# Batch 2's upper projections of the first layer as quadrant products, the sums of its weights one batch earlier

## The chip, the cores and the metric

One NeuronCore of a Trainium2 chip. The metric is device time of one execution, in microseconds. Before the change: 1840.14 us, median of 3 runs (1838.12 to 1842.43). The engines are called PE (TensorE, matmuls), ACT (ScalarE), DVE (VectorE), POOL (GpSimd) and SP (SyncE, which here issues nearly all DMAs).

## The reference

Windowed attention feeds two feed-forward layers; all in float32.

```
attention, 4 batches x 8 heads x 576 x 64   (window 32; heads 4..7 with dilation 4)
x  = heads side by side                                       2304 x 512
h  = max(max(x @ w1, x @ w2), x @ w3)                         2304 x 768
x2 = h @ w_out                                                2304 x 512
P  = 8 rounds of row and column scaling of exp(x2 @ w_gate)   2304 x 8
out = sum over 8 experts e of P[:, e] * (max(x2 @ v1[e], 0) @ v2[e])
```

The change touches the line with `h` alone, for batch 2 of the batches 0 to 3. The second layer (all from 394.9 us of the trace on) is left as it is.

## The kernel before

**Arithmetic.** Each float32 operand of a large product is split into a high and a low part: ACT casts the high part, DVE or POOL subtracts it from the source (`split`, line 97). A product is three passes, high x high, high x low, low x high (`PASS`, line 389), accumulated in PSUM.

**First layer, the plain way** (`up`, `up_step`, batches 0 to 2). A batch has 576 columns of x in two halves of 288, and 6 blocks of 128 rows of h. For each block, each half and each of the three weights there are 12 matmuls of 288 columns (4 pieces of the 512 inputs x 3 passes) into one of four PSUM buffers `ps_g`. ACT copies the first weight's product, DVE takes the maximum with the second's and the third's, and the result is split into `h1`. A raw tile `raw` holds two chunks of weights, each 128 x 512; for batch 2 they are fetched again (`fetch_next`) and split by ACT and POOL into tiles `wa` (`split_next`), one every two units from unit 82 on.

**First layer by quadrants** (`up_quads`, batch 3 alone). Two blocks of one weight and the two halves of x form 2 x 2 quadrants, and seven products of 6 matmuls replace eight. The seven need combined weights S1 to S4 and combined inputs T1 to T4. `sums_w1` makes S1 to S4 of the raw weights on DVE, four sums of 256 columns for each of the 9 pairs, in staging tiles, and stores them in DRAM (`wsf`); `more_w1` fetches them in groups of two pairs and splits them (X and Y), and fetches A11, A12 and A22, which batches 0 and 1 left split in DRAM (`wsp`). `make_quad` makes T1 to T4 of the input `xf` and splits all seven quadrants into the two large tiles `spaces`. A group of two pairs takes seven steps; in a step PE makes a product for each pair, 12 matmuls. `keep` copies a partial product out of PSUM (ACT), `result` adds it to another (DVE) and takes the running maximum over the three weights in `best`; the third weight's result is put on a list, `todo`, and split after the next step. Side 0 of a pair uses `ps_g`, side 1 the two buffers `pt`, which before that serve attention.

**Order.** A unit is one step of 12 matmuls; `hooks(unit)` (line 972) is called after each and issues what other work falls due there: attention of later batches (`BEGIN`, `PARTS`, `LATE`), sums of weights (`SUMS`: fetched five units ahead, two sums at the unit, two and the store at the next), the first group's weights (`FIRST`), the quadrants of x (`QUAD`). Units 56 to 79 are batch 1's upper projections, 80 to 87 its down projection, 88 to 123 batch 2's upper, 124 to 131 its down, 132 to 167 batch 3's upper. Batch 3's attention runs in batch 2's units; k and q of a pair of heads have one buffer each, loaded again when the scores before are done. PE's order is by hand throughout. From batch 1's down projection on, ACT's and DVE's order is by hand too; before it theirs, and always POOL's and SP's, is a planner's, which places instructions by its own simulated times and by their order in the program. Every engine works its queue in order.

**Buffers.** `raw` has 4, `wa` 8, `ps_g` 4, and `cx` 3, which hold in turn staging tiles, `xf`, `best` and `x2`.

Of the kernel before, what the change touches and what calls it, by code (L numbers as in the profile page):

```python
# [26 lines left out]
BEGIN = {2: (48, 60, 67, 71), 3: (91, 98, 105, 112)}  # L27
SUMS = (86, 89, 93, 96, 100, 103, 107, 110, 114)
WEIGHTS = 78
FIRST = {118: "S", 120: "A1", 121: "A2", 122: "X0", 123: "X1", 126: "Y0", 127: "Y1"}  # L30
LATE = {
    0: "S Ma", 1: "Mb", 2: "X0", 3: "X1", 4: "X2", 5: "X3", 6: "X4", 7: "Ra Rb", 8: "W",
    10: "T0 E0 T1 E1", 11: "T2 E2", 13: "V0 H0", 14: "V1 H1",
}
QUAD = {125: ("B11",), 126: ("T1",), 128: ("T2",), 129: ("B21",), 130: ("T3",), 132: ("B22",), 133: ("T4",)}
EARLY = {
# [80 lines left out]
def attention_moe(ctx: ExitStack, tc: tile.TileContext, q, k, v, mask, wm1, wg, wm2, out):  # L117
# [64 lines left out]
    def attn_ops(b, p, pool, qt, kt):  # L182
# [147 lines left out]
        for a in range(2):  # L330
            ops[f"V{a}"] = partial(v, a)
            ops[f"H{a}"], ops[f"L{a}"] = (partial(hi, a), partial(lo, a)) if b < 3 else (partial(whole, a), list)
        return ops
# [125 lines left out]
    wsf = dram.tile([NQ1, P, 2, 512], F32, name="wsf")  # L459
    stage, sums, raw_s, quads_w, best, raw_1 = [], {}, {}, {}, {}, {}  # L460
    groups = [[(3, i) for i in range(i0, min(i0 + 2, NQ1))] for i0 in range(0, NQ1, 2)]

    def fetch_next(g):
        raw_1[g] = fetch_w1(g)

    def split_next(j):
        t = w1_tile(j // 2)
        split(nc, t[:, 0], t[:, 1], raw_1[j // 2][:, j % 2], nc.gpsimd)
        made[2].append(t)

# [4 lines left out]
    def fetch_sums(i):  # L475
        if i < 4 and i % 2 == 0:
            stage.append(cx_p.tile([P, 2, 2, 512], F32, name="stage", tag="cx"))
        raw = sums[i] = stage[i // 2 % 2][:, i % 2]
        for j in range(2):
            nc.sync.dma_start(raw[:, j], chunk(i, j))  # L480
# [16 lines left out]
    def more_w1(g, what):  # L497

        group = groups[g] if g < len(groups) else ()
        if what[0] in "XY":  # L500
            k = int(what[1])
            if k >= len(group):
                return
            x = group[k]
            row, names, sub = (0, ("S2", "S4"), nc.gpsimd) if what[0] == "X" else (1, ("S3", "S1"), nc.gpsimd if g in (2, 3) else nc.vector)
            t = wa_p.tile([P, 2, 512], F32R, name="wa")
            split(nc, t[:, 0], t[:, 1], raw_s[x][:, row], sub)
            for c, name in zip((0, 256), names):
                quads_w[x][name] = halves_w(t, c)
            return  # L510
# [24 lines left out]

    def make_quad(name):

        x = xf[3]
        b11, b12, b21, b22 = (x[:, k:k + 2, n:n + HB] for k in (0, 2) for n in (0, HB))
        o, y, z = {  # L540
            "B11": (b11, None, None), "T1": (b11, b12, b11), "T2": (b11, b22, b11), "B21": (b21, None, None),
            "T3": (b12, b22, b12), "B22": (b22, None, None), "T4": (b21, b21, b11),
        }[name]
        if y is not None:
            nc.vector.tensor_tensor(out=o, in0=y, in1=z, op=ALU.subtract)
        t = quads_x[3, name] = quad(name)
        split(nc, t[:, 0], t[:, 1], o, nc.vector)

    def up_quads(g, unit):
# [14 lines left out]
        def product(k, side, w, x, first):  # L564
            if first:
                if side:
                    ps[k][side] = ps_a.tile([P, 512], F32, name="q", tag="pt", bufs=2)[:, :HB]
                else:
                    ps[k][side] = ps_g.tile([P, 512], F32, name="ps")[:, :HB]
            w, x = quads_w[group[k]][w], quads_x[b, x]  # L570
            n = 0
            for kk in range(2):
                for wi, xi in PASS:
                    nc.tensor.matmul(  # L574
                        ps[k][side], w[:, wi, kk], x[:, xi, kk], start=(first and n == 0),
                        stop=n == 5, skip_group_check=not first,
                    )
                    n += 1
# [19 lines left out]
        def after(n):  # L598
            nonlocal unit
            due = 7 * g + n + (n == 7 and g == len(groups) - 1)  # L600
            for _, op in [x for x in todo if x[0] < due]:
# [3 lines left out]
            if n == 1:  # L605
                more_w1(g, "Y1") if g else None
                more_w1(g + 1, "S")
            for what in {2: ("A1",), 4: ("A2",), 5: ("X0",), 6: ("X1",), 7: ("Y0",)}.get(n, ()):
                more_w1(g + 1, what)
            for _ in range((n + 1) // 2 - n // 2 if len(both) == 1 else 1 + (n == 7)):  # L610
# [361 lines left out]
    def hooks(unit):  # L972
# [14 lines left out]
        for i, u in enumerate(SUMS):  # L987
            if unit == u - 5:
                fetch_sums(i)
            if unit in (u, u + 1):  # L990
                sums_w1(i, unit - u)
        for what in FIRST.get(unit, "").split():
            more_w1(0, what)
        for late, step, op in ((0, 4, fetch_next), (4, 2, split_next)):
            i, now = divmod(unit - WEIGHTS - late, step)
            if 0 <= i < 36 // step and not now:
                op(i)
        for name in QUAD.get(unit, ()):
            make_quad(name)
        for what in EARLY.get(unit, "").split():  # L1000
# [12 lines left out]
    for what, unit in list(zip(WORK, starts))[done:]:  # L1013
# [8 lines left out]
        if f == "out":  # L1022
            down(b, unit)
            if b == B - 1:
                ordered.close()
        elif b == 3:
            if f == "0":
# [592 lines left out]
```

## Time and profile before

| | |
|---|---|
| median of 3 runs | 1840.14 us |
| the profiled execution | 1839.86 us, of which the span is 1838.1 us |
| PE busy | 1823.5 us (99%) |
| DVE, ACT, POOL busy | 1348.1 us (73%), 961.8 us (52%), 602.6 us (33%) |
| mean granted clock of PE | 0.995 of 2.4 GHz |
| DMA | 454.08 MB, mean 247 GB/s |
| batch 1 upper, batch 1 down | 154.4 to 204.5 us, to 227.0 us |
| batch 2 upper, batch 2 down | to 299.5 us, to 321.9 us |
| batch 3 upper, batch 3 down | to 374.3 us, to 394.9 us |

Times of rows are microseconds from the start of the span. A row of groups has: line, engine, operation, out<-in, shapes, count | busy us, mean ns of one | idle time of the engine before them, and what ended it. Matmuls overlap, so the mean of one is longer than the time from one to the next.

### The profile page before, as it was taken

How to read it: one execution, taken by the hardware profiler on the slowest of the kernel's cores; microseconds unless marked ns; L12 is line 12 of the kernel's file. 1: busy time of each engine (PE TensorE's matmuls, PEld its weight loads, DVE VectorE, ACT ScalarE, POOL GpSimd, SP SyncE). 2: the span in 40 equal slices, each digit the busy share in tenths (PEclk: the TensorE clock that was granted, in tenths of full speed). 3: DMA queues.
4: the chain of work that ended last, by engine and by line, in shares of the span. 5: the costliest groups of instructions: out<-in, count | busy, mean ns of one | idle time of the engine just before them, and what ended most of it. 6: DMA issues, size and time to landing. Idle time of an engine off the chain costs nothing.

```text
span 1838.1 us, 33541 instructions
## 1 busy us (share of the span) xinstructions
PE 1823.5 (99%) x11659; PEld 1703.1 (93%) x11659; DVE 1348.1 (73%) x2634; ACT 961.8 (52%) x2387; POOL 602.6 (33%) x536
## 2 busy tenths in 40 slices
PE   8999999999999999999999999999999999999999
PEld 6999999999999988899999999999999999999999
DVE  6884374768766677666597778877788777887777
ACT  6554454444554444544446555565555555565554
POOL 0013243336666677766512121121211211111211
PEclk8999999999999999999999999999999999999999
DMA  9678495866766678776977766777698676786773
GB/s 252 230 227 287 149 273 199 290 238 247 256 251 250 255 265 305 280 260 248 370 248 253 237 222 231 240 241 241 231 362 271 224 235 229 228 263 221 229 233 110
DMA packets 235369, 454.08 MB, mean 247 GB/s; under 512 B 38656, under 2 KB 121664, under 8 KB 233920
## 3 DMA queue, kind: packets, MB, share of 16 engines
q1 hardware_dynamic: 232240, 449.15, 72.4%
q10 hardware_dynamic: 2960, 2.79, 0.5%
q8 instruction: 93, 1.52, 0.3%
q14 instruction: 76, 0.62, 0.1%
HBM read 320.70 MB, written 130.81 MB: 246 GB/s over the span
## 4 chain that ended last, share of the span: by engine, by line
PE 75%; DVE 3%; DMA 1%; issue 1%; ACT 1%; POOL 1%; DVEq 0%; SPq 0%; POOLq 0%
PE po L1370 25%; PE po L1479 13%; PE po L1108 11%; PE p L1479 6%; PE q L1479 6%; PE p L1159 5%; PE q L1159 5%; PE ps L574 1%; DMA raw<-in_wm 1%; PE ps L652 1%; PE q L574 1%; DVE sums L839 1%; DVE ts L878 1%; DVE h L1212 1%; ACT h L1211 0%
## 5 line engine op out<-in xcount | busy, mean ns | idle before, releaser
L1370 PE MATMUL po<-wt,hop 128*128 128x512 f32 (+1 forms) x2772 | 469.7, 331 | 0.0
L1370 PEld LDWEIGHTS po<-wt,hop 128*128 128x128 f32 x2772 | 416.5, 188 | 51.0
L100 POOL TENSOR_TENSOR wt<-raw,wt 128x256 fp32r<-128x256 f32 x192 | 163.0, 874 | 757.8 <-ACT wt L99 677.1
L100 DVE TENSOR_TENSOR hop<-r,hop 128x384 fp32r<-128x384 f32 x384 | 210.5, 584 | 147.6 <-ACT hop L99 143.9
L1108 PE MATMUL po<-wb,h 128*128 128x512 f32 x1152 | 295.4, 392 | 0.4 <-POOL wb L100 0.4
L1108 PEld LDWEIGHTS po<-wb,h 128*128 128x128 f32 x1152 | 213.4, 188 | 33.9 <-POOL wb L100 1.0
L99 ACT CAST hop<-r 128x384 fp32r<-128x384 f32 x384 | 188.8, 516 | 50.0 <-DVE r L1346 28.2
L425 PE MATMUL ps<-xt,wa 128*128 128x288 f32 x1296 | 183.5, 298 | 0.0
L425 PEld LDWEIGHTS ps<-xt,wa 128*128 128x128 f32 x1296 | 173.5, 188 | 1.9
L100 POOL TENSOR_TENSOR wa<-raw,wa 128x256 fp32r<-128x256 f32 (+1 forms) x107 | 127.8, 1198 | 119.3 <-ACT wa L99 86.9
L1493 ACT ACTIVATE r<-r 128x384 f32<-128x384 f32 x192 | 97.8, 525 | 126.1 <-DVE r L1492 126.1
L1404 DVE SCALAR_TENSOR_TENSOR acc<-po,prob,acc 128x256 f32<-128x256 f32 x249 | 106.4, 478 | 17.3 <-PE po L1370 15.7
L100 POOL TENSOR_TENSOR tw<-ts,tw 128x512 fp32r<-128x512 f32 x64 | 87.2, 1382 | 91.7 <-DVE h L1212 59.1
L1479 PE MATMUL po<-xB,wa 128*128 128x384 f32 x576 | 115.5, 336 | 0.0
L1479 PE MATMUL po<-xt,wa 128*128 128x384 f32 x576 | 115.5, 336 | 0.0
L100 POOL TENSOR_TENSOR wa<-sums,wa 128x512 fp32r<-128x512 f32 x64 | 88.7, 1403 | 45.6 <-ACT wa L99 30.9
L1479 PEld LDWEIGHTS po<-xB,wa 128*128 128x128 f32 x576 | 101.3, 188 | 0.0
L1479 PEld LDWEIGHTS po<-xt,wa 128*128 128x128 f32 x576 | 101.3, 188 | 0.0
L100 POOL TENSOR_TENSOR wb<-raw,wb 128x512 fp32r<-128x512 f32 x64 | 93.0, 1453 | 23.7 <-ACT wb L99 23.2
L839 DVE TENSOR_TENSOR sums<-raw 128x256 f32<-128x256 f32 x64 | 46.3, 723 | 66.4 <-DMA raw<-in_wm 63.8
L1340 DVE TENSOR_TENSOR r<-r,r 128x384 f32<-128x384 f32 x128 | 93.2, 728 | 2.2
L1381 ACT COPY mm<-po 128x256 f32<-128x256 f32 x144 | 49.0, 376 | 73.5 <-PE po L1370 73.5
(239 smaller groups left out, 3318.6 us busy)
## 6 DMA issues: line engine op xcount, KB each, us to landing
wa<-wsd SPq DMA_DIRECT2D x192, 512.0 KB, 4.4
wt<-wtd SPq DMA_DIRECT2D x256, 256.0 KB, 3.6
wsd<-wa SPq DMA_DIRECT2D x96, 512.0 KB, 3.3
raw<-in_wm SPq DMA_DIRECT2D x64, 512.0 KB, 4.1
wtd<-tw SPq DMA_DIRECT2D x128, 256.0 KB, 2.7
raw<-in_wm SPq DMA_DIRECT2D x128, 256.0 KB, 5.2
wa<-wsd SPq DMA_DIRECT2D x64, 256.0 KB, 4.7
cx<-in_wm SPq DMA_DIRECT2D x10, 1024.0 KB, 7.2
```

The costliest lines, as they stand in the source:

```text
L99: nc.scalar.copy(hi, src)
L100: sub.tensor_tensor(out=lo, in0=src, in1=hi.bitcast(F32), op=ALU.subtract)
L425: nc.tensor.matmul(ps, w[:, wi, kk], xt[:, xi, kk, n0:n0 + HB], start=(n == 0), stop=(n == 3 * KT - 1),)
L839: nc.vector.tensor_tensor(out=s[:, o], in0=x, in1=y, op=op)
L1108: nc.tensor.matmul(po, self.hs[f, j][:, hi, t * P:(t + 1) * P], self.ws[f][:, wi], start=(n + f + k == 0), stop=(n == NPAIR - 1 and f == 1 ...
L1159: nc.tensor.matmul(ps, wo[w][:, wi, kk], xo[x][:, xi, kk], start=(first and k == 0), stop=True if k == 5 else False, skip_group_check=not ...
L1340: nc.vector.tensor_tensor(out=r[o, n], in0=r[x, n], in1=r[y, n], op=op)
L1370: nc.tensor.matmul(self.ps[side, t][:, 0:x.shape[-1]], h[:, hi, t * P:(t + 1) * P], x, start=(first and i == 0), stop=(n == NPAIR - 1 and ...
L1381: nc.scalar.copy(m, self.ps[ORD[k][0], t][:, 0:256])
L1404: nc.vector.scalar_tensor_tensor(out=a, in0=src, scalar=g, in1=a, op0=ALU.mult, op1=ALU.add)
L1479: nc.tensor.matmul(ps[k][side], wo[k][w][:, wi, kk], xo[x][:, xi, kk], start=(first and c == 0), stop=c == 5, skip_group_check=not first,)
L1493: nc.scalar.activation(out=r, in_=r, func=AF.Relu)
```

## The change

Batch 2's upper projections take the way of batch 3. The groups become ten, five for each batch. The sums of the weights are made at units 61 to 84 instead of 86 to 115, in `raw` tiles instead of staging tiles; the fetch and split of batch 2's plain weights goes. Batch 2's attention result is copied whole into `xf` and its quadrants are made at units 80 to 87. In batch 2 both sides of a pair use `ps_g`, and side 1 keeps its buffer for the group; all its weights' low parts are POOL's. An attention unit that fell after each 12 matmuls now falls after each step, and two after the seventh.

```
 BEGIN = {2: (48, 60, 67, 71), 3: (91, 98, 105, 112)}
-SUMS = (86, 89, 93, 96, 100, 103, 107, 110, 114)
-WEIGHTS = 78
-FIRST = {118: "S", 120: "A1", 121: "A2", 122: "X0", 123: "X1", 126: "Y0", 127: "Y1"}
+SUMS = (61, 64, 67, 70, 72, 75, 77, 80, 83)
+FIRST = {
+    0: {73: "S", 76: "A1", 77: "A2", 78: "X0", 79: "X1", 82: "Y0", 83: "Y1"},
+    5: {118: "S", 120: "A1", 121: "A2", 122: "X0", 123: "X1", 126: "Y0", 127: "Y1"},
+}
-QUAD = {125: ("B11",), 126: ("T1",), 128: ("T2",), 129: ("B21",), 130: ("T3",), 132: ("B22",), 133: ("T4",)}
+QUAD = {
+    2: {80: ("B11",), 81: ("T1",), 83: ("T2",), 84: ("B21",), 85: ("T3",), 86: ("B22",), 87: ("T4",)},
+    3: {125: ("B11",), 126: ("T1",), 128: ("T2",), 129: ("B21",), 130: ("T3",), 132: ("B22",), 133: ("T4",)},
+}
-            ops[f"H{a}"], ops[f"L{a}"] = (partial(hi, a), partial(lo, a)) if b < 3 else (partial(whole, a), list)
+            ops[f"H{a}"], ops[f"L{a}"] = (partial(hi, a), partial(lo, a)) if b < 2 else (partial(whole, a), list)
...
-    groups = [[(3, i) for i in range(i0, min(i0 + 2, NQ1))] for i0 in range(0, NQ1, 2)]
-
-    def fetch_next(g):
-        raw_1[g] = fetch_w1(g)
-
-    def split_next(j):
-        t = w1_tile(j // 2)
-        split(nc, t[:, 0], t[:, 1], raw_1[j // 2][:, j % 2], nc.gpsimd)
-        made[2].append(t)
+    groups = [[(b, i) for i in range(i0, min(i0 + 2, NQ1))] for b in (2, 3) for i0 in range(0, NQ1, 2)]
+    NG1 = len(groups) // 2
...
     def fetch_sums(i):
-        if i < 4 and i % 2 == 0:
-            stage.append(cx_p.tile([P, 2, 2, 512], F32, name="stage", tag="cx"))
-        raw = sums[i] = stage[i // 2 % 2][:, i % 2]
+        raw = sums[i] = raw_p.tile([P, 2, 512], F32, name="raw")
...
-            ... nc.gpsimd if g in (2, 3) else nc.vector)
+            ... nc.gpsimd if g < NG1 or g % NG1 in (2, 3) else nc.vector)
...
-    def make_quad(name):
+    def make_quad(b, name):
-        x = xf[3]
+        x = xf[b]
...
             if first:
-                if side:
+                if ps[k][side] is not None and b == 2:
+                    pass
+                elif side and b == 3:
                     ps[k][side] = ps_a.tile([P, 512], F32, name="q", tag="pt", bufs=2)[:, :HB]
                 else:
                     ps[k][side] = ps_g.tile([P, 512], F32, name="ps")[:, :HB]
...
-                more_w1(g, "Y1") if g else None
-                more_w1(g + 1, "S")
+                more_w1(g, "Y1") if g % NG1 else None
+                more_w1(g + 1, "S") if (g + 1) % NG1 else None
...
-        for late, step, op in ((0, 4, fetch_next), (4, 2, split_next)):
-            i, now = divmod(unit - WEIGHTS - late, step)
-            if 0 <= i < 36 // step and not now:
-                op(i)
...
-        elif b == 3:
+        elif b > 1:
```

## Rows read from the trace of the kernel before

**Rows 1.** The page, part 1: busy us (share of the span) and instructions.

```profile
PE 1823.5 (99%) x11659; PEld 1703.1 (93%) x11659; DVE 1348.1 (73%) x2634; ACT 961.8 (52%) x2387; POOL 602.6 (33%) x536
```

**Rows 2.** What PE waited for, 130 to 400 us: total, times, longest.

```profile
PE ps L574 <- ACT tmp L581: 0.5, 1, 0.5
PE pss L208 <- DMA qt<-in_q: 0.3, 1, 0.3
```

**Rows 3.** Stretches: length, busy us (instructions) by engine, PE clock, DMA share, GB/s.

```profile
154.40:204.50 50.10, 50.10 (x547) 48.61 (x546) 21.93 (x51) 25.12 (x95) 10.06 (x7) 1.00 0.54 173
204.50:227.00 22.50, 22.50 (x198) 22.26 (x197) 5.75 (x16) 7.13 (x19) 8.66 (x10) 1.00 0.64 216
227.00:299.50 72.50, 72.17 (x732) 69.56 (x730) 48.22 (x92) 38.03 (x135) 28.95 (x22) 1.00 0.82 253
321.90:374.30 52.40, 51.95 (x389) 51.28 (x388) 38.92 (x71) 25.32 (x62) 17.80 (x14) 1.00 0.76 263
```

**Rows 4.** PE's timeline, batches 2 and 3: start us, us, work, count.

```profile
252.73 0.82 PE L284 MATMUL pst<-ident,sm 128*96 128x128 f32 x6
253.30 1.85 PE L425 MATMUL ps<-xt,wa 128*128 128x288 f32 x12
...
258.61 0.80 PE L299 MATMUL pso<-pt,vt 96*64 96x64 f32 x20
...
261.75 1.04 PE L208 MATMUL pss<-kt,qt 64*64 64x96 f32 x36
...
276.16 1.34 PE L208 MATMUL pss<-kt,qt 64*64 64x96 f32 x36 [0.33 <-DMA qt<-in_q]
...
333.33 3.34 PE L574 MATMUL ps<-xt,wa 128*128 128x288 f32 x24
336.51 1.76 PE L574 MATMUL q<-xt,wa 128*128 128x288 f32 x12
```

**Rows 5.** Groups of ACT, 227.0 to 299.5 us.

```profile
L263 ACT ACTIVATE sm<-sm,st 128x96 f32<-128x96 f32 x36 | 13.3, 374 | 0.9 <-DVE st L250 0.9
L99 ACT CAST wa<-raw 128x512 fp32r<-128x512 f32 x16 | 9.9, 621 | 0.0
...
L287 ACT COPY pt<-pst 96x384 f32<-96x384 f32 x11 | 4.8, 476 | 1.1 <-PE pst L284 1.1
L435 ACT COPY tmp<-ps 128x288 f32<-128x288 f32 x12 | 4.7, 393 | 3.7 <-PE ps L425 3.7
```

**Rows 6.** Groups of DVE, 227.2 to 299.8 us.

```profile
L490 DVE TENSOR_TENSOR stage<-stage 128x256 f32<-128x256 f32 x34 | 24.3, 715 | 0.7
...
L438 DVE TENSOR_TENSOR tmp<-ps,tmp 128x288 f32<-128x288 f32 x12 | 5.5, 454 | 9.1 <-PE ps L425 9.1
```

**Rows 7.** Groups of DVE, 321.9 to 375.5 us (batch 3's upper projections).

```profile
L593 DVE TENSOR_TENSOR best<-best 128x288 f32<-128x288 f32 x9 | 6.5, 727 | 0.3
...
L589 DVE TENSOR_TENSOR best<-q,best 128x288 f32<-128x288 f32 x8 | 3.6, 451 | 0.4 <-PE q L574 0.2
```

**Rows 8.** Groups of DVE, 299.8 to 335 us: batch 3's quadrants of the input.

```profile
L100 DVE TENSOR_TENSOR xt<-xf,xt 128x576 fp32r<-128x576 f32 x7 | 5.6, 796 | 6.9 <-ACT xt L99 4.4 <-POOL xg L100 1.7 <-issue 0.8
...
L545 DVE TENSOR_TENSOR xf<-xf 128x576 f32<-128x576 f32 x4 | 3.0, 746 | 0.0
```

**Rows 9.** SP's timeline: the load of k for batch 3's last pair.

```profile
266.95 1.85 SPq L158 DMA_DIRECT2D kt<-in_k  x1
```

**Rows 10.** What SP's queue waited for, 150 to 300 us.

```profile
SPq L480 <- DMA wsf<-stage: 14.5, 5, 7.3
```

**Rows 11.** Groups of POOL, 227.0 to 299.5 us.

```profile
L100 POOL TENSOR_TENSOR wa<-raw,wa 128x512 fp32r<-128x512 f32 x16 | 20.8, 1306 | 33.3 <-ACT wa L99 22.2 <-PE pst L284 4.1 <-issue 3.7
```

**Rows 12.** Line 593 in batch 3: duration ns min/median/max, first and last start.

```profile
L593 DVE TENSOR_TENSOR best<-best x9: 459/461/1409, 327.3 to 367.7; 128x288 f32<-128x288 f32 x9
```

**Rows 13.** What PE waited for, 375 to 520 us.

```profile
PE p L1159 <- DVE h L1212: 0.3, 1, 0.3
```

**Rows 14.** Loads into `raw`, 100 to 230 us.

```profile
DMA to landing us min/median/max: 3.2/5.8/7.6
```

More of the change, by code (lines that the diff above doesn't have):

```diff
@@ L459, in attention_moe @@
     wsf = dram.tile([NQ1, P, 2, 512], F32, name="wsf")
-    stage, sums, raw_s, quads_w, best, raw_1 = [], {}, {}, {}, {}, {}
-    groups = [[(3, i) for i in range(i0, min(i0 + 2, NQ1))] for i0 in range(0, NQ1, 2)]
-    def fetch_next(g):
-        raw_1[g] = fetch_w1(g)
-    def split_next(j):
-        t = w1_tile(j // 2)
-        split(nc, t[:, 0], t[:, 1], raw_1[j // 2][:, j % 2], nc.gpsimd)
-        made[2].append(t)
+    sums, raw_s, quads_w, best = {}, {}, {}, {}
+    groups = [[(b, i) for i in range(i0, min(i0 + 2, NQ1))] for b in (2, 3) for i0 in range(0, NQ1, 2)]
+    NG1 = len(groups) // 2
     def chunk(i, j):
@@ L497, in more_w1 @@
     def more_w1(g, what):
-        group = groups[g] if g < len(groups) else ()
+        group = groups[g]
         if what[0] in "XY":
@@ L504, in more_w1 @@
             x = group[k]
-            row, names, sub = (0, ("S2", "S4"), nc.gpsimd) if what[0] == "X" else (1, ("S3", "S1"), nc.gpsimd if g in (2, 3) else nc.vector)
+            row, names, sub = (0, ("S2", "S4"), nc.gpsimd) if what[0] == "X" else (1, ("S3", "S1"), nc.gpsimd if g < NG1 or g % NG1 in (2, 3) else nc.vector)
             t = wa_p.tile([P, 2, 512], F32R, name="wa")
@@ L545, in make_quad @@
             nc.vector.tensor_tensor(out=o, in0=y, in1=z, op=ALU.subtract)
-        t = quads_x[3, name] = quad(name)
+        t = quads_x[b, name] = quad(name)
         split(nc, t[:, 0], t[:, 1], o, nc.vector)
@@ L599, in after @@
             nonlocal unit
-            due = 7 * g + n + (n == 7 and g == len(groups) - 1)
+            due = 7 * g + n + (n == 7 and g % NG1 == NG1 - 1)
             for _, op in [x for x in todo if x[0] < due]:
@@ L605, in after @@
             if n == 1:
-                more_w1(g, "Y1") if g else None
-                more_w1(g + 1, "S")
+                more_w1(g, "Y1") if g % NG1 else None
+                more_w1(g + 1, "S") if (g + 1) % NG1 else None
             for what in {2: ("A1",), 4: ("A2",), 5: ("X0",), 6: ("X1",), 7: ("Y0",)}.get(n, ()):
-                more_w1(g + 1, what)
+                more_w1(g + 1, what) if (g + 1) % NG1 else None
             for _ in range((n + 1) // 2 - n // 2 if len(both) == 1 else 1 + (n == 7)):
@@ L991, in hooks @@
                 sums_w1(i, unit - u)
-        for what in FIRST.get(unit, "").split():
-            more_w1(0, what)
-        for late, step, op in ((0, 4, fetch_next), (4, 2, split_next)):
-            i, now = divmod(unit - WEIGHTS - late, step)
-            if 0 <= i < 36 // step and not now:
-                op(i)
-        for name in QUAD.get(unit, ()):
-            make_quad(name)
+        for g, when in FIRST.items():
+            for what in when.get(unit, "").split():
+                more_w1(g, what)
+        for b, when in QUAD.items():
+            for name in when.get(unit, ()):
+                make_quad(b, name)
         for what in EARLY.get(unit, "").split():
```

## The prediction

> **What bounds the kernel now.** The page first: TensorE (PE) is busy 99% of the span [rows 1]. Then the list of what PE waited for from 130 to 400 us, that is from the end of batch 0 to the start of the second layer: two waits, 0.8 us together [rows 2]. Then the table of stretches: in batch 2's upper projections (227.0 to 299.5 us) PE is idle for 0.3 us, VectorE (DVE) is busy 48.2 of 72.5 us, ScalarE (ACT) 38.0 and GpSimd (POOL) 29.0 [rows 3]. So a matmul that goes there takes its time off the end, as long as nothing else comes to bind. What has to be asked of the change is therefore how many matmuls go, and which of the new small instructions PE must wait for.
>
> **What goes on PE.** Batch 2's upper projections are 6 blocks x 2 halves x 3 weights x 12 = 432 matmuls of 288 columns. By quadrants they are 9 pairs x 7 products x 6 = 378. 54 go. One costs what PE's timeline shows from start to start: 24 of batch 3's quadrant products fill the time from 333.33 to 336.51, 132.5 ns each [rows 4]. (The time that the timeline shows beside the count has the drain of the last one in it, which the next work overlaps.) 54 x 0.1325 = 7.2 us less. This is the one gain of the change that is on the path. Batch 3, which already works so, shows that such a stretch holds together: 378 products x 0.1325 = 50.1 us plus a few gate matmuls in a stretch of 52.4 us, with one wait of 0.5 us [rows 2, 3].
>
> **What is added beside it in batch 2.** (1) ACT. 24 evacuations (12 first copies, 12 high halves, about 0.4 us each) become 27 copies of partial products, 3 of finished ones and 12 high halves: 18 more x 0.39 = +7.0 us, so 45 of some 66.5 us, 68%. The 18 weight casts of 0.62 us are the same in number as the ones that go; four of them now fall ahead of the stretch, as batch 3's first do at its end [rows 5]. (2) DVE. The 36 sums of weights leave (34 in the stretch, 24.3 us), the 24 running maxima leave (two groups of 12, 5.5 us each) [rows 6]. In their place, at batch 3's durations, 27 sums of two products at 0.45 us (12.2), 18 maxima of two tensors in SBUF at up to 0.73 (13.1), 6 of a tensor in PSUM at about 0.45 (2.7) [rows 7]. 48.2 - 24.3 - 11.0 + 28.0 = 41 us of 66.5: less than now. (3) POOL: as many subtractions as before. (4) The input's quadrants: 4 differences of 0.75 us and 7 splits of 0.80 on DVE, 8.6 us, and as many casts on ACT [rows 8], all in batch 1's down projection (204.5 to 227.0), where DVE is busy 5.8 and ACT 7.1 of 22.5 us [rows 3]; together with the last eight sums of weights DVE has some 17 of 22.5 us there. Only the quadrant of the first product is needed at once, and it is made seven units before; the last is needed at the seventh product. Cost on PE: nothing; if it came late, its one split, 1.5 us.
>
> **Waits that it adds.** In batch 3 the second product of a pair has buffers of PSUM of its own; here all four partial sums of a group share the four `ps` buffers, so a group can only begin in what the last one gives back. Where the third weight's result stays in PSUM until it is split (`todo`, one product later), that split stands in ACT's queue behind the next group's own copies. I follow the worst hand-over, second to third group, from the end of the fourth product (t = 0). ACT then has, in its order: a copy 0.40, two exponentials, a weight cast 0.62, two exponentials, a cast, two evacuations of transposes at 0.48, two exponentials, a copy, a cast, the third evacuation, two exponentials, that is eight exponentials x 0.37 + 3 x 0.62 + 3 x 0.48 + 2 x 0.39 = 7.0 us [rows 5], and starts some 0.6 us late, for the first exponential needs a maximum that DVE still works on. Its next two copies and the split's high half (3 x 0.4) end at 8.8, DVE's low half at 9.3. PE meanwhile has three steps of 1.6, nine transposes (six take 0.57 from start to start, nine 0.8), a group's first step (1.6), 20 small matmuls of attention (0.7) and half a step (0.8), and then wants that buffer, at 8.7 [rows 4]. It waits 0.6 to 0.8 us; I take 0.8. The third to the fourth group has one pair of exponentials less before it and about a microsecond more of attention on PE, and comes out with nothing; the other hand-overs hold no split back. Within a group every buffer that is added to or overwritten has a whole step (1.6 us) between its reader's start and its next use, against 0.4 to 0.5 us a reader. For these I take what batch 3 shows, 0.5 us [rows 2]. Bounds: nothing at all on one side; on the other, ACT's lag of about 2 us at each of the four hand-overs, 8 us.
>
> **Loads of attention.** K and q of a head pair can only be loaded once the scores before them are done, for they have one buffer. Now the third pair's scores end at 262.8, the next k load starts at 266.95, and PE waits 0.33 us for q at 276.16 [rows 4, 9]: 4.2 us in SyncE's queue and 9.2 us to land. The change takes one step out of each such interval (a group has 7 products for 8 units of attention), about 2 us: 11 us would be left against 13.4. But the queue before that load was standing at loads of the sums' staging tiles, which wait for the store of the tile before (14.5 us in five waits) [rows 10]; these leave the stretch, and the loads of split weights that come wait for PE alone. By bytes it is even (20 loads and 9 stores of the sums go, 10 MiB with the fetches of raw weights; 7 sums, 7 first halves and 7 quarters come, 8.75 MiB). I take 0.3 us, that is no change from now; bounds: -0.3 (no wait) and +2.8 (2.6 at this load, 0.5 at the first).
>
> **Batch 1.** Seven of the nine pairs' sums move to its upper projections: 28 sums of 0.72 us, 20 us on a DVE that is busy 21.9 of 50.1 us, and 9 MiB more to move where the DMA share is 0.54 [rows 3, 6]. PE waits for nothing there now [rows 2]. Until the down projection the order of ACT, DVE, POOL and SyncE is the planner's, so I can't follow single instructions; I take 0.2 us, between 0 and the last rival's price.
>
> **A rule against it.** The 18 maxima with both inputs in SBUF are a new kind of work in this stretch, beside POOL's subtractions of 1.31 us [rows 11]. In batch 3 the nine of the largest group last 461 ns in the median and up to 1409 [rows 12]: now and then one stands for about as long as a POOL instruction. Their mean is 0.73, and that is what the sum has; a whole subtraction for each of them is rival B. The Trainium skill (SBUF — State Buffer, "Who interferes with whom") says that a VectorE instruction with two inputs in SBUF contends with a GpSimd one that reads SBUF, and that the second of the two fully blocks. The longest of the rows agrees with that, their median does not: most meet no such instruction. At its worst the rule would make rival B of it.
>
> **The sum**, against the profiled execution's 1839.86 us (span 1838.1 and 1.8 around it; the median of the runs is 1840.14): -7.2 + 0.8 + 0.5 + 0 + 0.2 = -5.7, so 1834.2 us. Its own range: all waits nothing, 1832; twice the waits and half the load's bound, 1837.
>
> **Rivals.** (A) ACT's lag is paid at every hand-over, 1 us at each of four instead of 0.8 once, and the steps behind it lose as much: +4 us, 1838. For it: ACT goes from 52% to 68% with its order fixed; against: batch 3 at 25.3 of 52.4 us waited once. (B) Each of the 18 maxima waits out a whole POOL subtraction: 18 x 1.31 = 24 us in place of 18 x 0.27, DVE at 60 of 66.5 us and late at most steps; evacuations set the pace, about +4 us: 1838. The median of 461 ns is against it. (C) The loads of k and q come late at their bound: 1837.2. (D) The gain is given back later: batch 3 or the second layer arrives 6 us sooner at something with its own clock (a load, the sums of w2). After 375 us PE waits for nothing but 0.3 us in the 145 us that follow [rows 13], but slack does not show in waits: 1839.9. (E) The slower one, one mechanism: the four `raw` buffers. The sums of weights, before in staging tiles of their own, now take `raw` buffers from the same four that feed batch 1's own weights, ahead of them in program order, each for a load (5.8 us), four sums (2.9) and a store (about as long as the load): 14 us. A pair of batch 1's weights that comes late holds PE for its load, cast and subtraction, 5.8 + 0.62 + 1.31 = 7.7 us [rows 5, 11, 14]. One late pair eats the gain (1842, the same by measurement); from the second on, at blocks 3 and 4, it decides: +15.4, 1849.6. Against it: nine tiles x 14 us are 126 us of four buffers' 200 in that stretch, and the planner loads far ahead.
>
> **Chances.** Forecast 0.66; A 0.12, B 0.04, C 0.05, D 0.06, E 0.07. 0.2% is 3.7 us (about what a measurement of this kernel can tell from no change): faster is below 1836.5, slower above 1843.8. Of the forecast's 0.66, 0.61 lie below 1836.5, and 0.05 of A and C: faster 0.66. D, most of A and B, the rest of C and of the forecast: the same, 0.28. Slower: E with two late pairs, 0.06. The range from 1831.5 to 1841.0 holds all but E and the tails of A and of the best case, 0.12 together; nearly all of its weight is on the faster side.
>
> **What would show it.** Right: a stretch of 378 quadrant matmuls for batch 2 of 65 to 68 us, PE idle in it 1 to 3 us with ACT or DVE lines 581 to 593 as releaser, the longest before the second product of the third group; batch 3 unchanged and everything behind it earlier by the same amount. Wrong: idle PE in batch 1 behind `wa` or `raw` (E), waits for k or q of over 1 us (C), DVE instructions of line 593 with a median near 1.4 us (B), waits of PE after 375 us that are not there now (D).

## The result: 1850.6 us, slower by 0.55%, and the profile after

The changed kernel takes 1850.63 us (median of 4 runs, 1846.60 to 1852.09) beside 1840.5 for the kernel before on the same chip: ratio 1.0055, 95% interval 1.0043 to 1.0068. The forecast was 1834.2, range 1831.5 to 1841.0. The profiled execution took 1852.09 us, span 1850.3.

The page, part 1, answers to [rows 1]: 54 matmuls fewer, and PE as busy as before.

```profile
PE 1823.7 (99%) x11605; PEld 1700.8 (92%) x11605; DVE 1364.3 (74%) x2658; ACT 973.8 (53%) x2412; POOL 604.2 (33%) x536
```

What PE waited for from 130 to 400 us (total, times, longest), where [rows 2] had two entries and 0.8 us: now 11.9 us.

```profile
PE ps L430 <- POOL wa L105: 2.4, 1, 2.4
PE pg L703 <- ACT xg L104: 2.2, 2, 1.5
PE ps L572 <- DVE h L105: 2.0, 1, 2.0
PE ps L430 <- ACT wa L104: 1.2, 1, 1.2
PE pg L703 <- POOL xg L105: 1.0, 2, 0.5
PE pg L703 <- DVE xt L105: 0.8, 1, 0.8
PE pss L213 <- DMA qt<-in_q: 0.7, 1, 0.7
PE pg L703 <- DVE sm L248: 0.6, 1, 0.6
PE pg L703 <- DVE xg L105: 0.5, 1, 0.5
PE ps L572 <- ACT tmp L579: 0.5, 1, 0.5
```

The stretches (columns as in [rows 3]): batch 0's down projection, batch 1's upper projections, batch 1's down projection, batch 2's upper projections. The last number but two is PE's clock.

```profile
133.10:158.20 25.10, 23.15 (x194) 21.76 (x193) 18.72 (x35) 9.61 (x32) 10.12 (x7) 1.00 0.86 298
158.20:215.10 56.90, 52.55 (x547) 50.35 (x546) 24.43 (x58) 27.94 (x100) 14.85 (x11) 0.97 0.93 309
215.10:242.06 26.96, 23.84 (x198) 22.63 (x197) 14.41 (x26) 9.04 (x22) 8.52 (x8) 0.98 0.65 227
242.06:313.00 70.94, 68.95 (x676) 66.03 (x676) 44.94 (x84) 44.99 (x153) 27.94 (x21) 0.93 0.72 214
```

Before, the four took 22.0, 50.1, 22.5 and 72.5 us. The last three are in [rows 3]; this is the first:

```profile
132.40:154.40 22.00, 22.00 (x194) 21.61 (x193) 12.20 (x24) 10.72 (x34) 12.19 (x9) 1.00 0.98 342
```

So batch 2's stretch won 1.6 us where 5.9 were forecast, and the three ahead of it, in which no PE instruction was added, lost 3.1, 6.8 and 4.5. Batch 2's down projection and batch 3 took what they took before (22.5, 52.5, 20.6 us). Four places, in order of time:

**Batch 0's down projection.** The planner put the first sums of weights here. DVE's timeline has them at 135.87, and POOL's has four subtractions in the same time:

```profile
135.87 4.81 DVE L486 TENSOR_TENSOR raw<-raw 128x256 f32<-128x256 f32 x4 [1.11 <-DMA raw<-wm1f]
```

```profile
134.83 5.57 POOL L105 TENSOR_TENSOR wa<-raw,wa 128x512 fp32r<-128x512 f32 x4 [17.50 <-DVE hx L450]
```

These four sums (one pair's) take 1.2 us each in the mean. Of the 12 in this stretch the median is 0.425 us and the longest 1.398, about one POOL subtraction (5.57 / 4 = 1.39). (The Trainium skill, SBUF — State Buffer, "Who interferes with whom", says that a VectorE instruction with two SBUF inputs contends with a GpSimd one that reads SBUF, and calls what they share an exclusive lock; these rows agree.) Copies out of PSUM and splits of x stand behind the sums on DVE, and PE waits three times for DVE, 1.8 us together. Over the rest of the 3.1 us the profile counts PE as busy with the same number of matmuls.

**Batch 1's upper projections.** SP's timeline shows the last pair of batch 1's weights (line 371) fetched at 193.95. In the kernel before the sixth load of batch 1's weights, which is its last, is issued here:

```profile
147.38 0.45 SPq L366 DMA_DIRECT2D raw<-wm1f  x1
```

In the changed kernel:

```profile
179.81 0.32 SPq L512 DMA_DIRECT2D raw<-wsf  x1
182.71 0.35 SPq L512 DMA_DIRECT2D raw<-wsf  x1
187.33 1.36 SPq L488 DMA_DIRECT2D wsf<-raw  x2
193.95 0.32 SPq L371 DMA_DIRECT2D raw<-wm1f  x1
```

The four `raw` buffers are full: two hold the raw weights of batch 2's first group (line 512, the step S of `FIRST`), two hold sums whose stores (line 488) have to land, and the first lands at 193.89. The program's own order leads there: the sums of units 75 and 77 are fetched at units 70 and 72, S falls at unit 73, and batch 1's last pair is asked for at unit 74, by the first step that needs it. It is the fifth tile in a ring of four, so it gets the buffer of the sum that is stored only at unit 76. The issue order in SP's timeline is the same. PE's timeline shows the price:

```profile
199.85 0.53 PE L430 MATMUL ps<-xt,wa 128*128 128x288 f32 x2 [1.17 <-ACT wa L104]
202.82 2.09 PE L430 MATMUL ps<-xt,wa 128*128 128x288 f32 x10 [2.44 <-POOL wa L105]
```

**Batch 1's down projection.** The rows of x2 are split into tiles `xg` for the gate products (line 703) and stored; there are two buffers. ACT's cast into one of them waited for the store of the tile that had the buffer before:

```profile
237.57 0.43 ACT L104 CAST xg<-x 128x288 fp32r<-128x288 f32 x1 [6.02 <-DMA x2s<-xg]
```

The view of the six stores that are issued in this stretch, first of the kernel before, then of the changed one:

```profile
DMA to landing us min/median/max: 2.6/2.9/3.1
```

```profile
DMA to landing us min/median/max: 2.6/3.8/8.1
```

Fetches of sums and weights for batch 2 are issued among them now.

**Batch 2, second to third group.** The wait for the late split is there, 1.99 us instead of 0.8, and at its end (275.35) the clock falls:

```profile
272.37 1.06 PE L572 MATMUL ps<-xt,wa 128*128 128x288 f32 x6
275.42 1.81 PE L572 MATMUL ps<-xt,wa 128*128 128x288 f32 x6 [1.99 <-DVE h L105]
```

Three stretches at the lower level, 1.2 of 2.4 GHz, none of which the kernel before has between 34 us and its end (columns as above):

```profile
203.70:207.10 3.40, 3.40 (x17) 3.31 (x16) 0.46 (x1) 0.95 (x2) 2.76 (x3) 0.50 1.06 372
241.20:244.60 3.40, 2.94 (x12) 2.94 (x13) 2.45 (x4) 1.33 (x4) 1.21 (x2) 0.50 0.72 190
275.30:282.20 6.90, 6.78 (x67) 6.16 (x68) 4.06 (x9) 1.45 (x6) 2.90 (x2) 0.51 0.79 252
```

In these 13.7 us PE is busy for 13.1. A matmul of 288 columns starts every 240 ns there (from 242.06 on) instead of every 132.5, so some 6 us are lost: an estimate, 13.1 x (1 - 132.5 / 240). That comes on top of 11.1 us more of waits; 7.2 us of matmuls are gone. Together this makes 9.8 of the 12.2 us between the two profiled spans; the rest is not accounted for.

### The profile page after: what moved, and what is told of

Same layout as the page of the kernel before. It is cut to its first block, busy times and chain, and to the rows that moved or that the text cites. A ratio compares the mean times of both kernels' runs of the same rounds, so it can differ in the third digit from the quotient of the medians.

```text
span 1850.3 us, 33532 instructions
## 1 busy us (share of the span) xinstructions
PE 1823.7 (99%) x11605; PEld 1700.8 (92%) x11605; DVE 1364.3 (74%) x2658; ACT 973.8 (53%) x2412; POOL 604.2 (33%) x536
## 4 chain that ended last, share of the span: by engine, by line
PE 74%; DVE 3%; DMA 2%; issue 1%; ACT 1%; POOL 0%; SPq 0%; DVEq 0%; ACTq 0%; POOLq 0%
PE po L1366 25%; PE po L1475 13%; PE po L1104 11%; PE q L1475 6%; PE p L1475 6%; PE q L1155 5%; PE p L1155 5%; DMA raw<-in_wm 1%; PE ps L650 1%; DVE sums L837 1%; PE ps L572 1%; DVE ts L876 1%; DVE h L1208 1%; PE q L572 1%; ACT h L1207 0%
## 5 line engine op out<-in xcount | busy, mean ns | idle before, releaser
L430 PE MATMUL ps<-xt,wa 128*128 128x288 f32 x864 | 123.3, 299 | 3.6 <-POOL wa L105 2.4
L430 PEld LDWEIGHTS ps<-xt,wa 128*128 128x128 f32 x864 | 116.6, 189 | 5.2 <-POOL wa L105 2.7
L572 PE MATMUL ps<-xt,wa 128*128 128x288 f32 x594 | 89.2, 304 | 2.4 <-DVE h L105 2.0
```

The costliest lines, as they stand in the source:

```text
L430: nc.tensor.matmul(ps, w[:, wi, kk], xt[:, xi, kk, n0:n0 + HB], start=(n == 0), stop=(n == 3 * KT - 1),)
L572: nc.tensor.matmul(ps[k][side], w[:, wi, kk], x[:, xi, kk], start=(first and n == 0), stop=n == 5, skip_group_check=not first,)
```

## The experiments

All fifteen in one table: four stretches of the profiled execution (start of the first matmul to that of the next stretch's, us), the median of the timed runs and its ratio to the kernel before on the same chip. Batch 2's stretch moves by a few us with how a hand-over falls. Where the profiled execution is not near the median, the text says so.

| kernel | b0 down | b1 up | b1 down | b2 up | us | ratio (95%) |
|---|---|---|---|---|---|---|
| before | 21.95 | 50.11 | 22.49 | 72.48 | 1840.5 | |
| changed | 25.13 | 56.92 | 26.94 | 70.96 | 1850.6 | 1.0055 (1.0043–1.0068) |
| e1_no_sums | 21.96 | 50.91 | 23.83 | 69.97 | 1840.2 | 0.9999 (0.9991–1.0008) |
| e2_stage | 21.82 | 53.06 | 26.77 | 69.73 | 1845.5 | 1.0026 (1.0015–1.0038) |
| e3_xg | 25.13 | 56.81 | 22.56 | 69.62 | 1846.1 | 1.0032 (1.0020–1.0044) |
| e4_split_now | 25.13 | 55.49 | 27.59 | 66.54 | 1849.0 | 1.0050 (1.0038–1.0062) |
| e5_hold | 25.13 | 57.03 | 27.08 | 70.81 | 1850.9 | 1.0064 (1.0052–1.0077) |
| e6_no_arith | 21.99 | 57.87 | 23.87 | 68.32 | 1844.5 | 1.0023 (1.0015–1.0032) |
| e7_spread | 25.13 | 58.35 | 22.46 | 71.44 | 1849.6 | 1.0054 (1.0042–1.0066) |
| e8_floor | 21.82 | 50.12 | 22.46 | 66.07 | 1834.9 | 0.9970 (0.9958–0.9982) |
| e9_pool | 21.82 | 61.81 | 22.46 | 65.84 | 1843.4 | 1.0012 (1.0001–1.0022) |
| e10_pool_late | 21.82 | 51.88 | 22.46 | 65.70 | 1836.9 | 0.9976 (0.9967–0.9985) |
| e11_raw5 | 22.69 | 50.60 | 22.47 | 64.41 | 1843.4 | 1.0024 (1.0015–1.0032) |
| e12_raw5_late | 22.53 | 54.39 | 22.47 | 65.83 | 1848.2 | 1.0044 (1.0033–1.0055) |
| e13_late | 25.12 | 50.07 | 22.88 | 72.97 | 1842.7 | 1.0013 (1.0004–1.0023) |
| e14_late_dve | 25.13 | 50.07 | 22.57 | 66.08 | 1837.7 | 0.9989 (0.9979–0.9998) |
| e15_first_pool | 22.31 | 51.11 | 22.61 | 66.42 | 1835.7 | 0.9980 (0.9971–0.9990) |

**The sums left out (e1_no_sums).**

```diff
-            if unit == u - 5:
-                fetch_sums(i)
-            if unit in (u, u + 1):
-                sums_w1(i, unit - u)
...
-                nc.sync.dma_start(raw, wsf[i])
+                nc.sync.dma_start(raw, wm1f[i])
```

> Left out: the sums of weights (their fetches, the 36 DVE instructions and the stores); batch 2's and 3's upper projections then read the plain upper weights where the sums stood, so the number and size of loads, casts and products there stay as they are. My theory: the moved sums cost about 10 us in batch 0's down projection (25.1 us against 22.0 before) and batch 1's upper projections (56.9 against 50.1), by holding two of the four raw buffers, DVE and the DMA; without them these two go back to 22.0 to 22.5 and 50 to 51 us, batch 1's down projection keeps most of its 4.5 us (batch 2's own loads are still there) and batch 2 its hand-over: 1840.5, between 1838 and 1843. Rival 1: the cost is in batch 2's fetches, quadrants and hand-over and the sums only happen to lie beside it: 1847 to 1851. Rival 2: it is the DMA as a whole, and with the sums' 9 MiB gone the down projection and the hand-over come right too: 1832 to 1835.

As expected for the time: the whole loss against before goes, and the hand-over (2.0 us and the half clock) stays. Not as expected, most of batch 1's down projection comes right too (23.83 us; "keeps most of its 4.5 us" was said). The rest of the study is about what in the sums costs 10 us.

**Sums staged elsewhere (e2_stage).** The kernel leaves out the waits of a staging tile's reload for the store before it: the fifth sum is fetched at 174.96 into the tile from which the third is stored at 182.93. Its time is without those waits.

```diff
-        raw = sums[i] = raw_p.tile([P, 2, 512], F32, name="raw")
+        if i < 2:
+            stage.append(h1_p.tile([P, 2, S], F32, name="stage", tag="h1"))
+        raw = sums[i] = stage[i % 2][:, :, 0:512]
```

> The sums are staged in two tiles of the pool of hidden rows, which batch 1 does not use, and no longer in the four raw buffers; same instructions, same units. If the raw buffers are the cause (the last pair of batch 1's weights is fetched at 193.95 in the changed kernel and holds PE for 3.6 us; 149.47 before), that wait and the clock's fall behind it go: batch 1's upper projections 51 to 53 us, 1844 to 1847. If it is DVE, or the DMA's load (share 0.93, a load landing after 8 us), it stays where it is: 1849 to 1852. If two tiles are too few, so that a fetch stands in SyncE's queue behind a store and batch 1's loads behind it, it is slower: 1853 or more.

53.06 us in batch 1 and 1845.5, as the buffers' theory had it: the waits for `wa` are gone at a DMA share of 0.95 (158 to 215 us; 0.93 in the changed kernel). That speaks for the buffers and against the DMA's load, but who holds them it can't tell.

**Four places for xg (e3_xg).** For batch 1 every third and fourth tile goes to a free part of `spaces[0]`.

```diff
+        elif b == 1 and i % 4 > 1:
+            n = 4 + i % 4
+            xg = spaces[0][:, n * 2 * HB:(n + 1) * 2 * HB].rearrange("p (s n) -> p s n", s=2)
```

> Batch 1's down projection gets four places for the split rows xg in place of two (two lie in the space that the first batch's rows left). If PE's 3.1 us of waits there come from the casts that wait for a store of the tile before (8 us to land instead of 3), they go, and the fall of the clock behind them: 27.0 to 22.5 or 23.5 us, 1846 to 1848. Rival: what is short is DVE and ACT (quadrants and sums in the same stretch), and the waits stay: 1849 to 1852.

The down projection is at 22.56 us and the time at 1846.1, as expected: with two places more PE does not wait there, though DVE and ACT have the same work. Where the buffers stay two, what PE pays for it varies: in e1 and e6 the casts still wait 7 us for stores and the stretch takes only 23.9 us.

**The last split early (e4_split_now).**

```diff
-            due = 7 * g + n + (n == 7 and g % NG1 == NG1 - 1)
+            due = 7 * g + n + (n == 7 and (b == 2 or g % NG1 == NG1 - 1))
```

> In batch 2's groups the last split of finished rows is put ahead of the next group's copies instead of one product later. If the hand-over from the second to the third group (PE waits 1.99 us for the low half, and then has the clock at half for 7 us) is the queue position of that split, 1.5 us of the wait and the 3.5 us of the half clock go: 1845 to 1847, batch 2's upper projections 66 to 67.5 us. Rival: ACT as such is behind, the copies of the next group come late instead, and the wait only changes its place: 1849 to 1852.

Batch 2's stretch comes to 66.54 us, and PE's only wait in it is this one:

```profile
PE pg L703 <- POOL xg L105: 0.3, 1, 0.3
```

The time came down by less than the stretch did, to 1849.0, outside the 1845 to 1847 that were expected: in the profiled execution the second layer's start gave 2.1 us back in one wait (line 1155 for ACT, which stood at a load of raw weights). In the profiles of e7 to e10, e14 and e15, which have the same edit, that wait is not there. The rest of the difference stays open.

**Sums held back (e5_hold).**

```diff
-SUMS = (61, 64, 67, 70, 72, 75, 77, 80, 83)
+SUMS = (64, 66, 68, 70, 72, 75, 77, 80, 83)
...
+                with tc.issue_after(mark[0].ins):
+                    sums_at(i, u, unit)
```

> The changed kernel with the sums' loads and arithmetic held back, so that the planner can't put them before the unit of batch 1 at which they are written (the first two at units 64 and 66 instead of 61 and 64). If batch 0's down projection grew from 22.0 to 25.1 us because the first four sums stand on DVE ahead of the split rows that PE waits for there, it goes back to 22 and 3 us come off: 1847 to 1848. Rival: all nine now fall into batch 1's upper projections, where the raw buffers and the DMA are the limit, and what is won in front is lost there: 1850 to 1853.

It failed as an experiment: `issue_after`, a hint to the planner (`mark[0]` is a cast of batch 1), left its order as it was, with the first sum's load at 132.33 (132.36 in the changed kernel). It is in effect a second run of that kernel and tells the theories in no way apart.

**Loads and stores, no arithmetic (e6_no_arith).**

```diff
-            nc.vector.tensor_tensor(out=o, in0=x, in1=y, op=op)
+            pass
```

> Left out: the 36 DVE instructions of the sums; their loads and stores, and the raw buffers that they hold, stay. It tells DVE from data movement. If buffers and DMA are the cause in batch 1, its upper projections keep 4 of their 6.8 us above before, and only batch 0's 3.1 us (DVE's order) goes: 1846 to 1848. If DVE is the cause in both, it is as without sums: 1840 to 1842.

The two causes come apart. Batch 0's down projection (first line) is right again, so its 3.1 us were DVE's; batch 1's (second line) is as long as in the changed kernel, with the same two waits for `wa` (3.6 us), so DVE is not the cause there. The time (1844.5) is lower than either theory had it, since batch 1's down projection came out at 23.87 us as well.

```profile
131.60:153.60 22.00, 22.00 (x195) 21.58 (x194) 11.69 (x23) 9.71 (x32) 9.81 (x7) 1.00 0.97 327
153.60:211.40 57.80, 52.89 (x546) 50.45 (x545) 18.84 (x42) 27.84 (x100) 14.90 (x11) 0.97 1.02 335
```

**Three remedies, sums spread (e7_spread).** The edits of e3 to e5, and `SUMS = (64, 66, 70, 74, 78, 90, 94, 98, 104)`.

> Three remedies in one, nothing left out: the sums held back and spread (five in batch 1's upper projections, four in batch 2's, at units 64, 66, 70, 74, 78, 90, 94, 98, 104), four places for xg in batch 1's down projection, and the last split of a group ahead of the next group's copies. By my theory each takes away its own wait: batch 0's down 22 us, batch 1's upper 51 to 53, its down 22.6, batch 2's upper 66.5 to 68 us, the rest as before: 1835.5 to 1838.5, under the kernel before. Rival 1: the sums in batch 2 (23 us of DVE with four of them put in its fixed order) hold back its evacuations: batch 2 at 70 us or more, 1840 to 1842. Rival 2: the five sums left are enough to starve batch 1 of raw buffers: its upper projections at 55 us, 1840 to 1843.

Wrong, and at 1849.6 outside the rivals' ranges too: the hint did nothing, so batch 0 stayed at 25.13 us, and both rivals' stretches came together. Batch 1 took 58.35 us, with ACT waiting 4.22 us for a late load of raw weights (rival 2's mechanism; S was at unit 73 here as well). Batch 2 took 71.44, rival 1's size, but by another way than DVE's order alone. There the sums now take `raw` buffers from batch 2's own groups: a cast on ACT waits 2.63 us for its load, the evacuations of transposes stand behind it, and PE waits 2.44 us for them; on DVE two sums take 2.64 us beside POOL.

**No sums, both remedies (e8_floor).** The edits of e1, e3 and e4.

> Left out: the sums of weights, as in the first experiment; with the two remedies for xg and for the last split. It shows what the quadrant products alone give. By my theory batch 2's upper projections take 66.5 us and batch 1's down projection 22.5, all else as before: 1840.2 - 3.5 - 1.3 = 1835.4, between 1834 and 1837, which is what I forecast for the change. Rival: batch 2's gain is given back at the start of the second layer (2.4 us of it were, in the profile of the experiment with the early split): 1838 to 1840.

As expected, 1834.9 (with the sums' loads and stores left out, so this is less work than the change needs). The stretches of batch 1 and batch 2:

```profile
155.40:205.50 50.10, 50.10 (x546) 48.65 (x545) 18.85 (x42) 26.77 (x98) 12.59 (x9) 1.00 0.69 205
205.50:228.00 22.50, 22.50 (x199) 22.26 (x198) 10.98 (x19) 9.46 (x23) 8.89 (x9) 1.00 0.62 211
228.00:294.10 66.10, 64.85 (x678) 62.38 (x676) 43.09 (x83) 44.31 (x152) 28.28 (x21) 1.00 0.74 220
```

**Sums on POOL (e9_pool); the first group later (e10_pool_late).** Both have the edits of e3 and e4 and the first of these; e10 also the second.

```diff
-            nc.vector.tensor_tensor(out=o, in0=x, in1=y, op=op)
+            nc.gpsimd.tensor_tensor(out=o, in0=x, in1=y, op=op)
...
-    0: {73: "S", 76: "A1", 77: "A2", 78: "X0", 79: "X1", 82: "Y0", 83: "Y1"},
+    0: {78: "S", 80: "A1", 81: "A2", 82: "X0", 83: "X1", 86: "Y0", 87: "Y1"},
```

> The changed kernel with the two remedies (four places for xg, the last split of a group early) and the sums' arithmetic on GpSimd (busy 15 of 57 us in batch 1) in place of DVE; loads, stores, buffers and units as in the changed kernel. If the sums' place on DVE is what lengthens batch 0's down projection (25.1 us, 22.0 without the arithmetic), that comes back, and batch 1's upper projections keep the wait for the last raw pair (3.6 us and the half clock behind it): 22.0, 55 to 57, 22.5, 66.5 us in the four stretches, 1840 to 1842. Rival: the sums on GpSimd delay the subtractions that PE waits for (some 25 us more on it): batch 1's upper projections 59 us or more, 1845.

> As the kernel with the sums on GpSimd, and the first group's loads, casts and subtractions for batch 2 five units later (S at 78 in place of 73, the rest in step). From S on two of the four raw buffers are held by batch 2's first group until its last cast; if that is what keeps batch 1's last pair waiting, its 3.6 us and the fall of the clock go: batch 1's upper projections 51 to 53 us, 1836 to 1838. Rival: the late casts crowd ACT and GpSimd in batch 1's down projection (quadrants, split rows) and PE waits there or at batch 2's first products for what it gained: 1840 to 1842. Rival: the sums themselves hold the buffers, no change from the run before: 1840 to 1842.

e9: batch 0's down projection comes right, batch 1's upper projections get worse (61.81 us, 4.9 of them in one wait for POOL's subtraction), so the rival had the stretch and, at 1843.4, not quite the time. e10, as expected: five units' delay of one group takes 9.9 us off batch 1's upper projections against e9, and the kernel is faster than e9 and, by 0.24%, than the kernel before. Its first two stretches:

```profile
133.20:155.10 21.90, 21.90 (x195) 21.62 (x194) 11.42 (x24) 9.68 (x32) 15.63 (x16) 1.00 0.93 317
155.10:206.90 51.80, 50.40 (x545) 48.74 (x545) 19.61 (x42) 26.85 (x98) 32.52 (x37) 1.00 1.03 354
```

**A staging tile for every second sum (e11_raw5, and with the late group e12_raw5_late).**

```diff
+    stage_p = tc.alloc_tile_pool(name="stage", bufs=1, side="right")
...
-        raw = sums[i] = raw_p.tile([P, 2, 512], F32, name="raw")
+        raw = sums[i] = (raw_p if i % 2 else stage_p).tile([P, 2, 512], F32, name="raw")
```

> As the kernel with the sums on GpSimd, with a staging tile of its own for every second sum (the room comes from the second xg buffer, whose tiles go to free places of the rows' spaces), so that four sums and not nine take raw buffers. If the raw buffers are the cause in batch 1's upper projections, the last pair comes in time: 51 to 53 us, 1836 to 1838. Rival: it is the DMA (8 us to land at a share of 0.93), and PE waits for weights or q as before: 55 us or more, 1840 to 1842.

> Both: the staging tile for every second sum and the first group of batch 2 five units later, with the two remedies and the sums on GpSimd. If buffers are all that is left, batch 1's upper projections take 50 to 52 us and the whole 1835 to 1837, what the kernel without sums and with the two remedies took (1834.9). Rival: the DMA's load sets a floor in batch 1 whatever the buffers (a k and q load, 8 us to land, 1 to 2 us of waits): 1837.5 to 1840.

In e11 batch 1's upper projections come right (50.60 us) with the group early: fewer sums in `raw` cure it too. But with a free buffer the planner fetches the first sum at 59.24, and batch 0's upper projections take 98.5 us in place of 90.5 (PE waits 4.5 us there for a load of v, and is at half the clock for 3.4 us). All expectations of the whole time were wrong for that. e12 has the same loss (97.1 us), and its batch 1 took 54.39 us where 50 to 52 were expected: 3.2 us of waits for q, as its rival had said, with 3.4 us at half the clock behind them.

**The late group alone (e13_late), and with the two remedies (e14_late_dve).** The edits are the line of FIRST in e10's diff alone, and that line with the edits of e3 and e4.

> The changed kernel with one edit: the first group of batch 2 is fetched, cast and split five units later (S at 78 in place of 73). If that group's two raw tiles are what keeps batch 1's last pair waiting, its 3.6 us and the half clock behind it go (batch 1's upper projections 52 to 53.5 us in place of 56.9), and the stores of xg in the down projection get out of the way of its loads or not (27 us as now, or 24): 1843 to 1847. Rival: the sums hold the buffers whatever the group does, 56 us or more, 1850 to 1852.

> The late group with the two remedies (four places for xg, early split), the sums on DVE as in the changed kernel. Against the same kernel with the sums on GpSimd (1836.9) it shows what the sums' place on DVE costs. By my theory batch 0's down projection is at 25.1 us again, where it was 21.8, and the rest is as there: 1839.5 to 1841, the same as the kernel before. Rival: DVE also holds back batch 1's casts and evacuations: 1842 to 1845. Rival: DVE costs nothing once the buffers are free: 1837.

The one line, put on the changed kernel, takes 8 us off the time (1842.7), a little more than expected. The last pair is fetched at 180.52 now, before S; batch 1's two stretches, in which PE waits for nothing:

```profile
180.52 0.32 SPq L371 DMA_DIRECT2D raw<-wm1f  x1
```

```profile
160.10:210.20 50.10, 50.10 (x548) 48.66 (x546) 24.37 (x58) 26.64 (x99) 12.42 (x9) 1.00 1.04 349
210.20:233.00 22.80, 22.80 (x197) 22.27 (x196) 14.02 (x26) 9.43 (x23) 9.18 (x9) 1.00 0.53 180
```

All nine sums, on DVE, and a DMA share of 1.04 (0.93 in the changed kernel) cost batch 1's upper projections nothing. The down projection is right too, but its two `xg` buffers are paid for later. In batch 2's first group PE waits 2.98 us for a copy on ACT, behind a cast that waits 2.75 us for a store of `xg`. (The profiled execution, 1847.1 us, is the slowest of twelve.) e14 came out 2 us better than my theory had it, 0.1% under the kernel before: batch 0's 3.1 us are there, but against e10 batch 1's upper projections are 1.8 us shorter. e10, with the sums on POOL, waits 1.4 us for a load of q there.

**The first two pairs' sums on POOL (e15_first_pool).** e14 with

```diff
-            nc.vector.tensor_tensor(out=o, in0=x, in1=y, op=op)
+            (nc.gpsimd if i < 2 else nc.vector).tensor_tensor(out=o, in0=x, in1=y, op=op)
```

> The late group and the two remedies, with the arithmetic of the first two sums on GpSimd and of the other seven on DVE. If these two, which the planner puts into batch 0's down projection, are the whole of its 3.1 us, it takes 21.8 to 22.2 us, and batch 1's upper projections 50.1 as with all on DVE (51.9 with all on GpSimd): about 1834.5, between 1833.5 and 1836. Rival: the third sum, which lies in the same stretch, or the GpSimd's two hold DVE back as much: 24 us or more there, 1837 to 1838.5.

Batch 0's down projection takes 22.31 us: those two were 2.8 of its 3.1 us. Batch 1's upper projections took 51.11 us and not 50.1, with 0.5 us of waits for q. The time is 1835.7, inside the range expected and level with e10 within the intervals, 0.2% under the kernel before and, by the two ratios, 0.75% under the changed one.

## Why the prediction was wrong, point by point

- **54 matmuls, 7.2 us: right.** With the waits beside it cured, batch 2's stretch is 65.7 to 66.4 us in the kernels that do all the work (e10, e14, e15; 65 to 68 was forecast), and the best of them takes 1835.7 beside a forecast of 1834.2. So the forecast's sum describes the change with its remedies and not the change.
- **"Batch 1 … I take 0.2 us": the step that failed.** It was priced by DVE's busy time and the DMA's share of the upper projections, which e6 and e13 show to be worth nothing there. The four `raw` buffers were what counted. Rival E had the resource, the 3.6 us of waits are about half of its 7.7, and it got 0.07. But it put a sum's hold of a buffer at 14 us, where the two in front of the last pair held theirs for 18 (load at 175.76 to landing at 193.89, and 177.08 to 195.12), and it put all on the sums. The change brings two claimants, the sums and the S of batch 2's first group, fetched in batch 1's time; I counted S only by its casts. Taking away either heals it (e1 and e11; e13). It cost 6.8 us: 3.6 of waits for `wa`, 0.7 for q, and some 1.5 by the fall of the clock behind them.
- **The same step left the planner's freedom open** ("I can't follow single instructions") and then looked only at the stretch for which the sums are written. For the buffers the program's order would have been enough: S at unit 73, the last pair at 74. The planner put three pairs' sums a stretch earlier, where DVE makes what PE waits for at once: 3.1 us, 2.8 of them from the first two pairs (e6, e15).
- **"Cost on PE: nothing" for batch 1's down projection: wrong by 4.5 us,** and for a reason outside the sum. DVE had room, as I said (14.4 of 27 us busy); the two `xg` buffers had none, since their stores go through the DMA beside what is fetched for batch 2 (e3). In the kernel before they landed after 3 us and hid this. Moving the fetches later does not take the place of buffers: e13 pays 2.98 us for them in batch 2.
- **The hand-over, 0.8 us: right place, wrong size.** 1.99 us, and then 6.9 us at the lower clock, some 3 us more; e4 took 4.4 us off the stretch. The bounds (0 to 8) held it, but they were made of ACT's lag and not of the clock.
- **The loads of k and q in batch 2: inside the bounds.** PE waits for none of them there in the changed kernel, where 0.3 us was taken; the 0.7 us for q in the list lie in batch 1's upper projections (at 192.32), where none was forecast. Once the hand-over is cured (e8), PE waits 1.3 us for q in batch 2, more than the sign that was given for rival C. Rival B: the nine maxima have a median of 0.945 us in the changed kernel and 0.458 in e8. That fits their meeting POOL, which no run tests, but PE's only wait for DVE in that stretch is the split. DVE is busy 44.9 us there, where 41 was forecast. Rival A did not come (one hand-over waits). Of D there is the 2.1 us in e4.
- **The clock** stood in no step: each wait was priced at its length.

## What to carry to other kernels

Before moving loads into an earlier stretch, list every claimant of each small buffer pool there with the times that it takes and frees a buffer, stores included; busy shares and DMA shares say nothing of that. A prefetch that is merely early can cost more than the work that it feeds: here one line, five units later, was worth 8 of 10 us. Where the buffers of a small pool are handed out in program order, count back from the load that is needed first by as many tiles as there are buffers, and ask when that tile is given back. And where a planner orders an engine, follow the moved work to where it may be put, not to where it is written.

## What the hardware showed that I had not expected

- The clock fell to half at the end of a single wait of PE of 1.99 us (at 275.35), and after waits of 1.51, 0.47 and 0.66 us within 5 us, as a fourth began (at 241.21, down projection of batch 1), and 0.8 us behind waits of 1.17 and 2.44 us (at 203.67). It stayed there for 6.8, 3.4 and 3.4 us. But length alone does not decide it: after single waits of 2.37 us (for q at 191.78 in e9), 2.1 (e4) and 1.4 (e10) it did not fall. By the pace of the matmuls (240 ns in place of 132.5) 3.4 us at half the clock lose some 1.5 us and 6.8 some 3, about 0.4 to 1.5 times the waits before them, on top of these.
- DMA engines that are busy all the time need not cost PE anything: 349 GB/s at a share of 1.04 with no wait of PE (e13), 309 at 0.93 with 4.3 us of them (the changed kernel).
- DVE's sums of 256 columns took 0.41 to 0.43 us while POOL was idle and up to 1.40 beside POOL's subtractions; one took 1.83 beside another instruction of POOL (at 179.74 in e7).
